# Seven products for the third quarter of an attention output, with block sums, z sums and layer norm scales put elsewhere

## The chip, the cores and the metric

One core of a Trainium2 chip. The metric is the device time of one execution in microseconds (us), the median of several runs; lower is better. TensorE (PE) multiplies matrices, VectorE (DVE) and ScalarE (ACT) do elementwise work, GpSimd (POOL) does some of it too, SyncE (SP) issues the DMAs. The engines run in parallel, each works off its own queue in order, and they wait for each other by semaphores.

## The reference

Four residual layers on x of shape (1, 2048, 1024): attention, GLU, attention, GLU with the same weights in both rounds.

```python
x = x + A(layernorm(x)); x = x + B(layernorm(x))
x = x + A(layernorm(x)); x = x + B(layernorm(x))

# A: 32 heads of 32; phi(t) = where(t > 0, t + 1, exp(t)) + 1e-6
pq, pk = phi(q), phi(k)
kv = einsum("bhsd,bhse->bhde", pk, v); z = einsum("bhsd->bhd", pk)
o = einsum("bhqd,bhde->bhqe", pq, kv) / (einsum("bhqd,bhd->bhq", pq, z)[..., None] + 1e-6)
A = o @ wo
# B: F = 3584
B = (relu(x @ W_gate) * (x @ W_up)) @ W_down
```

## The kernel before

The 2048 tokens are 16 tiles of 128 rows in four quarters of four (QT = 4). The class runs layer_A(0, 1), layer_B(1), layer_A(2, 3), layer_B(3). Layer A makes phi(k), phi(q) and kv, and folds the weight wo into kv (fold_wo): T is then 1024x1024 in bf16, and a tile's attention output is its phi(q), divided by its z sums and transposed (pqT), times T. out_unit (L773) does one tile and one half of the columns: eight matmuls of 128x512 into one bank of the pool `ps` (PSUM, 4 banks), then one DVE instruction (add_up, L768) that adds the residual and gathers the row's sum for the next layer norm. Quarters 0, 1 and 2 go by out_unit, 8 units each, 24 in a layer. Quarter 3 goes by out_pairs (L787): seven block products, Strassen's, for a pair of row tiles against a pair, 56 matmuls in place of 64, with four block sums of T (sums_T, more_T: 128x2048 each) and four of pqT (sums_q: 128x1024). In before they are made while GLU steps u=1 and u=2 of layer B run, and the products follow step u=2.

Around the out stage:

- z sums: for each of 16 tiles z_mult (L723, POOL), z_sum (L728 to L730, DVE: reduce, add, reciprocal), z_scale (L735, POOL), then the transposing DMA q_turn (L744, SP).
- The layer norm of layer B's first half (tiles 0 to 7, ln_norm_sums): L222 on DVE, square, Ln, Exp, shift and scale on ACT (L225 to L231), a transposing DMA (ln_turn, L410), then sums_x (L1127 to L1130, DVE) for four pairs of tiles, which the fifth of the GLU's seven products (`five`, bank vg, L1154) needs.
- make_gu (L1064 to L1067, DVE) makes block sums of a GLU weight; in layer 1 they are stored to DRAM for later (L1068).
- In layer 2 the layer norm's root (ln_root, L173 and L174, ACT) and scale (L180, DVE) lie among the products of q and k.

The order: each unit or product calls later.tick(); later.at(n, f) runs f after n more ticks, and so puts its instructions at that place of the program. In the out stage DVE and POOL keep the program's order (manual_schedule); elsewhere a scheduler orders by its own costs, and issue_after(i) or behind(i, f) keep a step behind instruction i. The order of the out stage in before:

```python
for i in range(11, self.ST):
    later.at(1 + 3 * (i - 11), lambda i=i: z_mult(*divmod(i, QT)))
self.ln_later(last_ln, 0, 2, 2, 2)
run(out0[3:])
for sc in range(1, self.NQ - 1):
    ...
    run(row_major(out_unit, sc))
```

Of the kernel before, what the change touches and what calls it, by code (L numbers as in the profile page):

```python
# [92 lines left out]
class _Net:  # L93
    def __init__(self, tc, ctx, x_d, wqkv_d, wo_d, wg_d, wu_d, wd_d, out_d):
# [23 lines left out]
        self.small = pool("small", 4)  # L118
        self.ps = pool("ps", 4, space=PSUM)
# [64 lines left out]
    def ln_norm(self, layer, t):  # L184
# [14 lines left out]
        def scale(rstd=None if layer == 2 else rstd):  # L199
            if rstd is None:  # L200
                rstd = self.ln_root(mv)
                return lambda: scale(rstd)
# [12 lines left out]
    def ln_norm_sums(self, layer, t):  # L215
# [13 lines left out]
        def scale():  # L229
            nc.scalar.activation(out=shift, in_=mean, func=ACT.Identity, scale=rstd[:, 0:1])  # L230
            nc.scalar.activation(out=xn, in_=src, func=ACT.Identity, scale=rstd[:, 0:1],  # L231
                                 bias=shift[:, 0:1])
            return xn
# [178 lines left out]
    def ln_at(self, delay, layer, t, lag, after=None):  # L412
        def stat():
            with self.tc.issue_after(after) if after else nullcontext():
                scale = self.ln_norm(layer, t)
# [15 lines left out]
    def phi(self, ps, out):  # L431
# [4 lines left out]
        nc.scalar.activation(out=e, in_=e, func=ACT.Exp, scale=-1.0, bias=self.eps6[:, 0:1])  # L436
# [30 lines left out]
    def layer_A(self, l, last_ln):  # L467
# [89 lines left out]
        def m_products(q_first):  # L557
# [39 lines left out]
            later.at(2 if l else 6, lambda: z_chain(0))  # L597
# [118 lines left out]
        def z_chain(i):  # L716
            z_mult(*divmod(i, QT))
            if i < 10:
                later.at(2 + i % 2, lambda: z_chain(i + 1))

        def z_mult(sc, j):
            prod = ksum
            nc.gpsimd.tensor_tensor(out=prod, in0=pq_of[sc, j], in1=zrow, op=ALU.mult)  # L723
            later.at(2, lambda: z_sum(prod, sc, j))

        def z_sum(prod, sc, j):
            den = self.small.tile([P, D // HD], F32, tag="den")
            nc.vector.tensor_reduce(out=den, in_=heads(prod), axis=mybir.AxisListType.X, op=ALU.add)  # L728
            nc.vector.tensor_scalar(out=den, in0=den, scalar1=1e-6 * self.mean, scalar2=None, op0=ALU.add)
            nc.vector.reciprocal(out=den, in_=den)  # L730
            later.at(2, lambda: z_scale(den, sc, j))

        def z_scale(den, sc, j):
# [3 lines left out]
                in1=den[:, :].unsqueeze(2).to_broadcast([P, D // HD, HD]), op=ALU.mult)  # L737
# [49 lines left out]
        def out_pairs(sc):  # L787


            nc, P2 = self.nc, 2 * P  # L790
# [4 lines left out]
            def sums_T():  # L795
                W = self.slot(f"sT{l}", [P, 2, 4, NW], F16)
                S["R"] = R = self.slot(f"sR{l}", [P, 2, 4, NW], F16)
                S[1], S[2], S[4] = W[:, 0], W[:, 1], R[:, 0]
                op(S[1], b12, b11)
                op(f16(b12), b22, b12)  # L800
                later.at(4, more_T)

            def more_T():
                op(S[2], b22, S[1])
                op(S[4], b21, S[2])

            def sums_q():
                q = pqT[sc]
                a11, a12, a21, a22 = (q[:, h:h + 4, i * P2:(i + 1) * P2] for i in range(2) for h in (0, 4))
                s1 = self.temp([P, 4, P2], F16, name="s1")  # L810
                s2, s4 = (S["R"][:, 1, i * 2:i * 2 + 2, :].rearrange("p a (b n) -> p (a b) n", n=P2)
                          for i in range(2))
                op(s1, a21, a22, ALU.add)
                op(s2, s1, a11)
                op(f16(a21), a11, a21)
                op(s4, a12, s2)
                if l == 0:
                    with self.tc.issue_after(self.last_relu.ins):
                        for t in range(sc * QT, sc * QT + QT):
                            for n in range(2):  # L820
                                nc.scalar.activation(out=half(self.x[t], n), in_=half(self.xb[t], n),
                                                     func=ACT.Copy)
# [3 lines left out]
            def products():  # L826
                X = [self.ps.tile([P, NW], F32, tag="a", name=f"ox{i}") for i in range(2)]
                V = [self.ps.tile([P, NW], F32, tag="a", name=f"ov{i}") for i in range(2)]
                Y = [self.ps3.tile([P, NW], F32, tag="b", name=f"oy{i}") for i in range(2)]

                def onto(i, n, bank, last):
                    xs = half(self.x[sc * QT + i], n)
                    if last:
                        add_up(sc * QT + i, n, xs, bank, xs)
                    else:
                        nc.vector.tensor_tensor(out=xs, in0=xs, in1=bank, op=ALU.add)
# [718 lines left out]
```

## Time and profile before

| what | value |
|---|---|
| median of 3 runs | 1448.07 us (1447.98 to 1448.23) |
| profiled execution | 1447.77 us |
| its span, first to last instruction | 1446.0 us |
| granted TensorE clock | 1.000 |
| matmuls | 7430 |
| out stage of layer 0, layer 2 | about 174 to 214 us, 892 to 932 us |

A group's line gives the source line, engine, operation, names, shapes and count, then busy us and mean ns of one, then the idle time before them and what ended it. A window's line gives the stretch, its length, the busy us (and count) of PE, its weight loads, DVE, ACT and POOL, the clock, the DMA share and GB/s. A line of the chain or timeline gives start and duration in us.

### The profile page before, as it was taken

To read this page: it belongs to the slowest core of one execution; us is meant where nothing else is said; L and a number is where in the kernel's file an instruction comes from. 1 tells how busy PE (TensorE), PEld (TensorE's weight loads), DVE (VectorE), ACT (ScalarE), POOL (GpSimd) and SP (SyncE) were. 2 spreads that over 40 slices of the span, in tenths; PEclk is the share of its full clock that TensorE was granted. 3 is DMA by queue.
4 is the path that set the end of the run, shared out by engine and by line. 5 is a ranking of instruction groups with operands and counts; after the bars stand their busy time and mean duration, and the time that the engine had idled before them with its cause. 6 is when DMAs were issued, how large, how long until landed. Compare 5 with 4: busy or idle time off the path is not lost.

```text
span 1446.0 us, 20268 instructions
## 1 busy us (share of the span) xinstructions
PE 1437.7 (99%) x7430; PEld 709.2 (49%) x7430; DVE 959.7 (66%) x1799; ACT 613.8 (42%) x1113; POOL 309.6 (21%) x221
## 2 busy tenths in 40 slices
PE   9999999999999999999999999999999999999998
PEld 4444444444455444445654444444444574444457
DVE  7978698677594456549687885764445864444595
ACT  7872564233334334332168726633333433333300
POOL 1453861011100011110031586410111011111002
PEclk9999999999999999999999999999999999999999
DMA  9950787997469999646973119968644799444465
GB/s 287 237 161 8 176 212 204 288 333 255 162 213 288 355 307 307 202 127 220 297 253 88 58 30 266 261 233 269 217 146 130 220 293 323 146 146 146 153 234 181
DMA packets 328836, 304.90 MB, mean 211 GB/s; under 512 B 107456, under 2 KB 291776, under 8 KB 327712
## 3 DMA queue, kind: packets, MB, share of 16 engines
q1 hardware_dynamic: 320688, 282.30, 65.8%
q10 hardware_dynamic: 6560, 17.24, 3.1%
q0 software_dynamic: 1488, 4.07, 0.8%
q8 instruction: 58, 0.95, 0.3%
q14 instruction: 42, 0.34, 0.1%
HBM read 227.28 MB, written 51.64 MB: 193 GB/s over the span
## 4 chain that ended last, share of the span: by engine, by line
PE 92%; DVE 5%; ACT 1%; issue 1%; DMA 1%; SPq 0%; DVEq 0%; ACTq 0%
PE yu L1154 10%; PE yg L1154 10%; PE ps L493 10%; PE dy L1267 8%; PE xu L1154 6%; PE xg L1154 6%; PE dx L1267 6%; PE ps L776 4%; PE zu L1154 3%; PE vg L1154 3%; PE vu L1154 3%; PE zg L1154 3%; PE my L575 3%; PE dyT L1319 2%; PE mv L575 2%; PE mx L575 2%
## 5 line engine op out<-in xcount | busy, mean ns | idle before, releaser
L1154 PEld LDWEIGHTS <-w 128*128 128x128 f16 (+1 forms) x3136 | 306.7, 98 | 372.4 <-issue 3.6
L1207 POOL TENSOR_TENSOR h<-m5u,m5g 128x512 f16<-128x512 f32 x56 | 72.7, 1298 | 721.1 <-DVE m5u L1203 660.0
L493 PE MATMUL ps<-w,xnT 128*128 128x512 bf16 x768 | 169.9, 379 | 0.5 <-ACT xnT L348 0.3
L1190 DVE TENSOR_TENSOR zg<-yg,m5g 128x512 f32<-128x512 f32 x56 | 39.1, 699 | 180.2 <-PE yg L1154 176.1
L493 PEld LDWEIGHTS <-xnT 128*128 128x128 bf16 x768 | 74.4, 98 | 90.0 <-issue 1.6
L1154 PE MATMUL yg<-s,w 128*128 128x512 f16 x448 | 115.0, 379 | 0.3 <-DVE zg L1190 0.3
L1154 PE MATMUL yu<-s,w 128*128 128x512 f16 x448 | 114.9, 379 | 0.1
L1154 PE MATMUL xu<-xnT,w 128*128 128x512 f16 x448 | 115.0, 379 | 0.0
L1154 PE MATMUL xg<-xnT,w 128*128 128x512 f16 x448 | 115.0, 379 | 0.0
L1267 PEld LDWEIGHTS <-h 128*128 128x128 f16 x672 | 65.7, 98 | 78.3
L1162 ACT ACTIVATE m5g<-m5g 128x512 f32<-128x512 f32 x56 | 35.2, 628 | 155.0 <-DVE m5g L1203 155.0
L1319 PEld LDWEIGHTS <-h 128*128 128x128 f16 x966 | 94.5, 98 | 12.3
L436 ACT ACTIVATE e<-e,eps 128x512 f32<-128x512 f32 x128 | 91.0, 720 | 3.2
L723 POOL TENSOR_TENSOR kvc<-pq,kvc 128x1024 f32<-128x1024 bf16 x32 | 78.5, 2454 | 53.1 <-DVE den L728 32.8
L1267 PE MATMUL dx<-w,h 128*128 128x512 bf16 x392 | 85.3, 379 | 0.0
L776 PE MATMUL ps<-T,pqT 128*128 128x512 bf16 x384 | 83.6, 379 | 0.0
L1171 ACT ACTIVATE m5g<-vg 128x512 f32<-128x512 f32 x56 | 33.4, 597 | 108.5 <-PE vg L1154 108.5
L1165 DVE TENSOR_TENSOR h<-yu,r 128x512 f16<-128x512 f32 x56 | 38.7, 691 | 52.8 <-PE yu L1154 52.8
L514 POOL TENSOR_TENSOR kvc<-kvc,slab 128x512 f32<-128x512 f32 x46 | 57.2, 1249 | 76.0 <-DVE slab L439 72.7
L1162 ACT ACTIVATE r<-yg 128x512 f32<-128x512 f32 x56 | 33.4, 597 | 85.2 <-PE yg L1154 85.2
L1203 DVE TENSOR_TENSOR m5u<-yu,m5u 128x512 f32<-128x512 f32 x56 | 38.7, 690 | 46.3 <-PE yu L1154 46.3
L435 ACT ACTIVATE e<-ps 128x512 f32<-128x512 f32 x92 | 54.2, 589 | 28.9 <-PE ps L493 28.8
(234 smaller groups left out, 2385.5 us busy)
## 6 DMA issues: line engine op xcount, KB each, us to landing
w<-in_B_W_gate_dram SPq DMA_DIRECT2D x56, 512.0 KB, 6.1
w<-in_B_W_up_dram SPq DMA_DIRECT2D x56, 512.0 KB, 6.0
w<-tg SPq DMA_DIRECT2D x42, 512.0 KB, 7.3
w<-tu SPq DMA_DIRECT2D x42, 512.0 KB, 6.6
w<-ddT SPq DMA_DIRECT2D x21, 896.0 KB, 6.5
w<-td SPq DMA_DIRECT2D x18, 896.0 KB, 5.0
w<-dd SPq DMA_DIRECT2D x15, 896.0 KB, 5.0
w<-in_B_W_down_dram SPq DMA_DIRECT2D x14, 896.0 KB, 4.9
```

The source lines that it names most:

```text
L435: nc.scalar.activation(out=e, in_=ps, func=ACT.Relu, scale=-1.0)
L436: nc.scalar.activation(out=e, in_=e, func=ACT.Exp, scale=-1.0, bias=self.eps6[:, 0:1])
L493: nc.tensor.matmul(by_row(ps), lhsT=self.xnT[l, l_q][:, kt, j * P:(j + 1) * P], rhs=w[:, kt, :].rearrange("p (b i d) -> p i b d", i=R, d=H ...
L514: nc.gpsimd.tensor_tensor(out=ksum[:, cols], in0=ksum[:, cols], in1=pk, op=ALU.add)
L575: nc.tensor.matmul(banks[j], lhsT=A(i)[:, j * P:(j + 1) * P], rhs=B(i), start=start and i == 0, stop=i == NS - 1, skip_group_check=True)
L723: nc.gpsimd.tensor_tensor(out=prod, in0=pq_of[sc, j], in1=zrow, op=ALU.mult)
L776: nc.tensor.matmul(ps, lhsT=pqT[sc][:, g, j * P:(j + 1) * P], rhs=T[g // 4][:, g % 4, n2 * NW:(n2 + 1) * NW], start=(g == 0), stop=(g == G ...
L1154: nc.tensor.matmul(ps, lhsT=W[w][m][:, k, :], rhs=A[m][:, k, :], start=start and k == 0, stop=k == 3, skip_group_check=True)
L1162: self.last_relu = nc.scalar.activation(out=out, in_=ps, func=ACT.Relu)
L1207: nc.gpsimd.tensor_tensor(out=h[:, 3, :], in0=V["u"], in1=V["g"], op=ALU.mult)
L1267: nc.tensor.matmul(banks[j], lhsT=A(k)[:, j * P:(j + 1) * P], rhs=w[:, i, :], start=start and k == 0, stop=k == self.U - 1, skip_group_che ...
L1319: nc.tensor.matmul(bank[:, j * H:(j + 1) * H], lhsT=A[i // 2][:, i % 2, j * P:(j + 1) * P], rhs=B[m][:, i, :], start=start and i == 0 and ...
```

## The change

- Quarter 2 also goes by seven products (products(2, 1)) in each attention layer. The order of the products becomes 1, 5, 2, 6, 3, 7, 4. In layer 0 the residual is read from the input tile, with a temporary `held` for one half, in place of copies of x by ACT.
- Three of the block sums of T are made in quarter 0 of the out stage, the fourth ahead of the products; the sums of pqT of quarter 2 in quarter 1.
- The chain of z sums runs from tile 0 to 13; those of tiles 14 and 15 go into the GLU's first step (late_z). Offset and reciprocal are done for two tiles at once.
- The layer norm scale of tiles 4 to 7 is one tensor_scalar on POOL; one of the four sums in sums_x is on POOL for the first half of layers 1 and 3. Tile 7's layer norm is issued behind the products' last copy on ACT.
- make_gu for the first step at ticks 2 and 6 of quarter 1 (3 and 11 before), the later ones apart from each other, their stores behind the last relu. The first GLU step exchanges two pairs of PSUM banks (swap). The transposes and loads of quarter 3 move to u=1 in both layers. The layer norm roots of layer 2 are issued behind the last Exp of phi.

```diff
--- before.py
+++ after.py
...
+        self.den = pool("den", 2)
...
@@ -198,7 +199,8 @@

         def scale(rstd=None if layer == 2 else rstd):
             if rstd is None:
-                rstd = self.ln_root(mv)
+                with self.tc.issue_after(self.last_exp.ins):
+                    rstd = self.ln_root(mv)
                 return lambda: scale(rstd)
...
@@ -227,6 +229,10 @@
         nc.scalar.activation(out=rstd, in_=rstd, func=ACT.Exp, scale=-0.5)

         def scale():
+            if QT <= t < 2 * QT:
+                nc.gpsimd.tensor_scalar(out=xn, in0=src, scalar1=mean, scalar2=rstd[:, 0:1],
+                                        op0=ALU.add, op1=ALU.mult)
+                return xn
...
+            it = after() if callable(after) else after
+            with self.tc.issue_after(it) if it else nullcontext():
...
-        nc.scalar.activation(out=e, in_=e, func=ACT.Exp, scale=-1.0, bias=self.eps6[:, 0:1])
+        self.last_exp = nc.scalar.activation(out=e, in_=e, func=ACT.Exp, scale=-1.0, bias=self.eps6[:, 0:1])

...
-            later.at(2 if l else 6, lambda: z_chain(0))
+            later.at(2 if l else 4, lambda: z_chain(0))
...
@@ -715,26 +722,37 @@

         def z_chain(i):
             z_mult(*divmod(i, QT))
-            if i < 10:
+            if i < self.ST - 3:
                 later.at(2 + i % 2, lambda: z_chain(i + 1))
...
-            later.at(2, lambda: z_sum(prod, sc, j))
+            if (sc, j // 2) == (self.NQ - 1, 1):
+                later.at(2, lambda: self.behind(self.last_z, lambda _: z_sum(prod, sc, j), (0,)))
+            else:
+                later.at(2, lambda: z_sum(prod, sc, j))
+
+        dens = {}

         def z_sum(prod, sc, j):
-            den = self.small.tile([P, D // HD], F32, tag="den")
-            nc.vector.tensor_reduce(out=den, in_=heads(prod), axis=mybir.AxisListType.X, op=ALU.add)
-            nc.vector.tensor_scalar(out=den, in0=den, scalar1=1e-6 * self.mean, scalar2=None, op0=ALU.add)
-            nc.vector.reciprocal(out=den, in_=den)
-            later.at(2, lambda: z_scale(den, sc, j))
+            n, odd = D // HD, j % 2
+            if not odd:
+                dens[sc, j // 2] = self.den.tile([P, 2 * n], F32, tag="den", name="den")
+            den = dens[sc, j // 2]
+            nc.vector.tensor_reduce(out=den[:, odd * n:(odd + 1) * n], in_=heads(prod),
+                                    axis=mybir.AxisListType.X, op=ALU.add)
+            if odd:
+                nc.vector.tensor_scalar(out=den, in0=den, scalar1=1e-6 * self.mean, scalar2=None, op0=ALU.add)
+                nc.vector.reciprocal(out=den, in_=den)
+                for i in range(2):
+                    later.at(2 + 2 * i, lambda i=i: z_scale(den[:, i * n:(i + 1) * n], sc, j - 1 + i))
...
@@ -784,70 +802,72 @@
...
-        def out_pairs(sc):
-
-
...
-            def sums_T():
-                W = self.slot(f"sT{l}", [P, 2, 4, NW], F16)
-                S["R"] = R = self.slot(f"sR{l}", [P, 2, 4, NW], F16)
-                S[1], S[2], S[4] = W[:, 0], W[:, 1], R[:, 0]
-                op(S[1], b12, b11)
-                op(f16(b12), b22, b12)
-                later.at(4, more_T)
-
-            def more_T():
-                op(S[2], b22, S[1])
-                op(S[4], b21, S[2])
-
-            def sums_q():
+            def sums_T(n):
+                if n == 0:
+                    W = self.slot(f"sT{l}", [P, 2, 4, NW], F16)
+                    S["R"] = R = self.slot(f"sR{l}", [P, 2, 4, NW], F16)
+                    S[1], S[2], S[4] = W[:, 0], W[:, 1], R[:, 0]
+                out, a, b = ((S[1], b12, b11), (S[2], b22, S[1]), (S[4], b21, S[2]), (f16(b12), b22, b12))[n]
+                op(out, a, b)
+
+            def sums_q(sc, ns=range(4)):
                 q = pqT[sc]
                 a11, a12, a21, a22 = (q[:, h:h + 4, i * P2:(i + 1) * P2] for i in range(2) for h in (0, 4))
-                s1 = self.temp([P, 4, P2], F16, name="s1")
+                if 0 in ns:
+                    S["s1"] = self.temp([P, 4, P2], F16, name="s1")
+                s1 = S["s1"]
                 s2, s4 = (S["R"][:, 1, i * 2:i * 2 + 2, :].rearrange("p a (b n) -> p (a b) n", n=P2)
                           for i in range(2))
-                op(s1, a21, a22, ALU.add)
-                op(s2, s1, a11)
-                op(f16(a21), a11, a21)
-                op(s4, a12, s2)
-                if l == 0:
-                    with self.tc.issue_after(self.last_relu.ins):
-                        for t in range(sc * QT, sc * QT + QT):
-                            for n in range(2):
-                                nc.scalar.activation(out=half(self.x[t], n), in_=half(self.xb[t], n),
-                                                     func=ACT.Copy)
+                for n in ns:
+                    op(*((s1, a21, a22, ALU.add), (s2, s1, a11), (f16(a21), a11, a21), (s4, a12, s2))[n])
...
-            def products():
+            def products(sc, ticks):
...
-                def onto(i, n, bank, last):
-                    xs = half(self.x[sc * QT + i], n)
-                    if last:
-                        add_up(sc * QT + i, n, xs, bank, xs)
+                held = {}
+
+                def onto(i, n, bank, m):
+                    t = sc * QT + i
+                    xs = half(self.x[t], n)
+                    x0 = half(self.xb[t], n) if l == 0 and m not in (7, 3) else xs
+                    if l == 0 and m == 5:
+                        held[i] = self.temp(name="held")
+                    if m == 7:
+                        x0 = held.get(i, xs)
+                    out = held[i] if i in held and n == 1 else xs
+                    if m in (5, 6):
+                        nc.vector.tensor_tensor(out=out, in0=x0, in1=bank, op=ALU.add)
                     else:
-                        nc.vector.tensor_tensor(out=xs, in0=xs, in1=bank, op=ALU.add)
-
-                for m, bank, start, n in ((1, X, True, None), (5, V, True, (2, 1)), (6, Y, False, (0, 1)),
-                                          (2, X, False, (0, 0)), (7, Y, False, (2, 1)),
-                                          (3, V, False, (0, 1)), (4, Y, False, (2, 0))):
+                        self.last_x = add_up(t, n, out, bank, x0)
+                    if m == 4 and l == 0:
+                        later.at(6, lambda: self.behind(self.last_relu, lambda _: nc.scalar.activation(
+                            out=half(self.x[t], 1), in_=held[i], func=ACT.Copy), (0,)))
+
+                for m, bank, start, n in ((1, X, True, None), (5, V, True, (2, 1)), (2, X, False, (0, 0)),
+                                          (6, Y, False, (0, 1)), (3, V, False, (0, 1)),
+                                          (7, Y, False, (2, 1)), (4, Y, False, (2, 0))):
...
-                            nc.scalar.activation(out=Y[i], in_=X[i], func=ACT.Copy)
+                            self.last_seed = nc.scalar.activation(out=Y[i], in_=X[i], func=ACT.Copy).ins
                         else:
-                            onto(n[0] + i, n[1], bank[i], m not in (5, 6))
-                        later.tick()
+                            onto(n[0] + i, n[1], bank[i], m)
+                        if i or ticks == 2:
+                            later.tick()
...
@@ -943,27 +963,31 @@
...
-            for i in range(11, self.ST):
-                later.at(1 + 3 * (i - 11), lambda i=i: z_mult(*divmod(i, QT)))
+            sums_T, sums_q, products = out_pairs()
+            for n, at in enumerate((1, 3, 5)):
+                later.at(at, lambda n=n: self.behind(self.last_x, sums_T, (n,)))
             self.ln_later(last_ln, 0, 2, 2, 2)
             run(out0[3:])
             for sc in range(1, self.NQ - 1):
                 if sc == 1:
                     for j in range(QT):
-                        self.ln_at(2 * j + 2, last_ln, QT + j, 2)
-                        later.at((11 if l else 12, 13, 15, 16)[j], lambda j=j: self.sums_x(last_ln, 0, j))
-                if sc == 2 and l:
-                    for j in range(QT):
-                        later.at(11 + j, lambda j=j: q_turn(self.NQ - 1, j))
-                    for t in range(self.ST - QT, self.ST):
-                        later.at(3 + t, lambda t=t: self.behind(self.last_turn, bring, (t,)))
+                        self.ln_at((2, 4, 6, 9)[j], last_ln, QT + j, 2, lambda j=j: self.last_seed if j == 3 else None)
+                        later.at((11 if l else 12, 13, 15, 16)[j], lambda j=j: self.behind(
+                            self.last_x, lambda j: self.sums_x(last_ln, 0, j), (j,)))
                 if sc == 1 and l == 0:
-                    for w, n in (("g", 3), ("u", 11)):
+                    for w, n in (("g", 2), ("u", 6)):
                         later.at(n, lambda w=w: self.behind(
                             self.last_x, lambda w: self.make_gu(ring.get((last_ln, 0, w, 0)), w, 0), (w,)))
-                run(row_major(out_unit, sc))
-            self.pairs = out_pairs(self.NQ - 1)
-            self.turns = [] if l else [lambda j=j: q_turn(self.NQ - 1, j) for j in range(QT)] + [
+                if sc == 1:
+                    for n in range(4):
+                        later.at(3 + n, lambda n=n: self.behind(self.last_x, lambda n: sums_q(2, (n,)), (n,)))
+                    run(row_major(out_unit, sc))
+                else:
+                    self.behind(self.last_x, sums_T, (3,))
+                    products(sc, 1)
+            self.pairs = lambda: sums_q(self.NQ - 1), lambda: products(self.NQ - 1, 2)
+            self.late_z = [lambda j=j: z_mult(self.NQ - 1, j) for j in (2, 3)]
+            self.turns = [lambda j=j: q_turn(self.NQ - 1, j) for j in range(QT)] + [
                 lambda t=t: self.behind(self.last_turn, bring, (t,)) for t in range(self.ST - QT, self.ST)]


...
-        self.later.at(3, lambda: self.nc.scalar.dma_start(
-            out=self.tgu[w, u], in_=t[:, 4:8, :].bitcast(F16)))
+
+        def store():
+            with self.tc.issue_after(self.last_relu.ins) if u else nullcontext():
+                self.nc.scalar.dma_start(out=self.tgu[w, u], in_=t[:, 4:8, :].bitcast(F16))
+
+        self.later.at(3, store)
...
-        v.tensor_tensor(out=s3, in0=a11, in1=a21, op=ALU.subtract)
+        self.last_s3 = (self.nc.gpsimd if c == 0 and l % 2 else v).tensor_tensor(out=s3, in0=a11, in1=a21, op=ALU.subtract)
         v.tensor_tensor(out=s4, in0=a12, in1=s2, op=ALU.subtract)
...
+        swap = c == 0 and u == 0
+
+        def bank(w, third, name):
+            if third:
+                return self.ps3.tile([P, NW], F32, tag="b", name=name)
+            return self.kvp.tile([P, NW], F32, tag="kv0" if w == "g" else "kv1", name=name)
+
         def five(w):
-            v = self.kvp.tile([P, NW], F32, tag="kv0" if w == "g" else "kv1", name=f"v{w}")
+            v = bank(w, swap, f"v{w}")
             mm(w, 5, v, True)
...
-            Y[w] = self.ps3.tile([P, NW], F32, tag="b", name=f"y{w}")
+            Y[w] = bank(w, not swap, f"y{w}")
...
-                        self.later.at(4 if u else 9, lambda u=u: behind(self.last_put if u else self.last_z, lambda: [
-                            self.make_gu(ring.get((l, c, w, u + 1)), w, u + 1) for w in "gu"]))
+                        for n, w in enumerate("gu"):
+                            self.later.at((4 if u else 9) + 4 * n, lambda u=u, w=w: behind(
+                                self.last_put if u else self.last_z,
+                                lambda: self.make_gu(ring.get((l, c, w, u + 1)), w, u + 1)))
...
+                if c == 0 and u == 0:
+                    for n, z in enumerate(self.late_z):
+                        self.later.at(7 + 3 * n, lambda z=z: behind(self.last_s3, z))
                 if c == 0 and u == 1:
                     for n, turn in enumerate(self.turns):
-                        self.later.at(1 + n, turn)
-                if c == 0 and u in (1, 2):
-                    self.later.at(6, lambda u=u: behind(self.last_put, self.pairs[u - 1]))
+                        self.later.at(7 + n + 6 * (n // QT), turn)
+                if c == 0 and u == 2:
+                    self.later.at(6, lambda: behind(self.last_put, self.pairs[0]))
                 self.glu(l, c, u, hT)
                 if c == 0 and u == 2:
-                    self.pairs[2]()
+                    self.pairs[1]()
...
```

More of the change, by code (lines that the diff above doesn't have):

```diff
@@ L413, in stat @@
         def stat():
-            with self.tc.issue_after(after) if after else nullcontext():
+            it = after() if callable(after) else after
+            with self.tc.issue_after(it) if it else nullcontext():
                 scale = self.ln_norm(layer, t)
@@ L736, in z_scale @@
                 out=heads(pq), in0=heads(pq),
-                in1=den[:, :].unsqueeze(2).to_broadcast([P, D // HD, HD]), op=ALU.mult)
+                in1=den.unsqueeze(2).to_broadcast([P, D // HD, HD]), op=ALU.mult)
             if sc < self.NQ - 1:
@@ L784, in out_unit, with out_pairs @@
             self.last_x = add_up(t, n2, xs, ps, x0)
-        def out_pairs(sc):
-            nc, P2 = self.nc, 2 * P
+        def out_pairs():
+            P2 = 2 * P
             f16 = lambda a: a.bitcast(F16)
```

## The prediction

> **What bounds the kernel now.** I read the page's busy lines and chain first, then windows over the stages the change touches (layer 0: 174 to 222 us, layer 2: 890 to 938), then the groups of instructions there by shape, the timeline where a group's mean looked wrong, and the chain again at PE's few stalls. The page:
>
> ```profile
> span 1446.0 us, 20268 instructions
> ...
> PE 1437.7 (99%) x7430; PEld 709.2 (49%) x7430; DVE 959.7 (66%) x1799; ACT 613.8 (42%) x1113; POOL 309.6 (21%) x221
> ...
> PE 92%; DVE 5%; ACT 1%; issue 1%; DMA 1%; SPq 0%; DVEq 0%; ACTq 0%
> ```
>
> TensorE is busy all but 8 us, so a matmul removed is time removed, provided that no other engine becomes late in that stage. The windows (span in us, then busy us of PE, PEld, DVE, ACT and POOL) show how near that is:
>
> ```profile
> 174.00:192.00 18.00, 18.00 (x96) 8.11 (x88) 15.54 (x39) 11.17 (x22) 17.38 (x9) 1.00 0.80 178
> 192.00:209.00 17.00, 17.00 (x80) 7.70 (x79) 16.19 (x35) 15.60 (x32) 12.20 (x7) 1.00 0.78 185
> 209.00:222.00 13.00, 12.76 (x59) 5.58 (x58) 11.43 (x32) 2.96 (x5) 0.00 (x0) 1.00 1.06 241
> 890.00:910.00 20.00, 20.00 (x107) 8.88 (x106) 13.62 (x38) 13.76 (x27) 11.09 (x7) 1.00 1.12 271
> 910.00:925.00 15.00, 15.00 (x71) 6.83 (x70) 11.46 (x32) 14.81 (x31) 10.91 (x7) 1.00 1.11 256
> ```
>
> DVE is busy 31.7 of the 35 us from 174 to 209, POOL 97% of the first window: in layer 0 there is hardly room on DVE, in layer 2 some. What fills them, DVE and then POOL, 174 to 222 us:
>
> ```profile
> L768 DVE SCALAR_TENSOR_TENSOR x<-ps,x 128x512 f32<-128x512 f32 x24 | 15.9, 669 | 1.5 <-PE ps L776 1.1
> L728 DVE TENSOR_REDUCE den<-kvc 128x32 f32<-128x1024 f32 x7 | 8.5, 1214 | 0.1
> L1064 DVE TENSOR_TENSOR w<-w 128x1024 f16<-128x1024 bf16 x2 | 4.5, 2256 | 0.0
> ...
> L735 POOL TENSOR_TENSOR pq<-pq,den 128x1024 bf16<-128x1024 bf16 x8 | 15.3, 1911 | 0.7 <-DVE den L730 0.7
> L723 POOL TENSOR_TENSOR kvc<-pq,kvc 128x1024 f32<-128x1024 bf16 x7 | 14.9, 2127 | 5.9 <-DVE den L728 5.9
> ```
>
> The same L1064, and the block sums that the change moves, 222 to 250 us:
>
> ```profile
> L1064 DVE TENSOR_TENSOR w<-w 128x1024 f16<-128x1024 bf16 x6 | 3.9, 683 | 0.0
> ...
> L546 DVE TENSOR_TENSOR sT<-T 128x2048 f16<-128x2048 bf16 x1 | 1.2, 1219 | 0.0
> ...
> L546 DVE TENSOR_TENSOR s<-pqT 128x1024 f16<-128x1024 bf16 x1 | 0.7, 682 | 0.0
> ```
>
> One shape, 0.68 us in one place and 2.26 in the other. The timeline says why:
>
> ```profile
> 192.39 1.91 POOL L735 TENSOR_TENSOR pq<-pq,den 128x1024 bf16<-128x1024 bf16 x1
> 192.47 2.38 DVE L1064 TENSOR_TENSOR w<-w 128x1024 f16<-128x1024 bf16 x1
> ```
>
> The DVE sum ends 0.55 us after POOL's multiply ends (194.30): it did not move until then. The other one (206.93, 2.13 us) lies over POOL's 206.61 to 208.52 in the same way. Reduces (1214 ns) and additions out of PSUM (669) under POOL are not longer than alone.
>
> Last, the stalls of PE. The chain from 748 to 755 us in layer 2:
>
> ```profile
> 749.14 0.29 ACT rstd L173
> ...
> 750.01 0.67 ACT e L436
> ...
> 752.06 1.02 PE qy L677 x4
> ```
>
> PE lost 1.19 us before 752.06 (distance of matmul starts over their usual 0.216). An Ln of a layer norm, waiting for its mean, held ACT and with it the exponential that DVE and PE needed. At 217.83 PE lost another 0.40, at vg, waiting for L1127 of tile 7.
>
> [...] The two-input multiplies of 128x1024 take 1.91 and 2.12 here; no row shows a one-input operation on POOL.
>
> **The change part by part.**
> *Seven products.* Eight units of eight matmuls become 56: eight fewer per layer. Eight take 1.727 us (pitch 215.8 ns), so −1.73 twice, −3.45. This is the sure part. DVE's results become 12 of 0.61 in place of 8, 2.4 us more, after unit 16.
>
> *The DVE queue of layer 0 up to unit 16.* The first addition starts at 175.7. An addition costs 0.61 with its accumulator read (the chain gives 1.22 for two). To the end of the 16th: 16 additions 9.8; four reduces at 1.14 4.6; two merged offset-and-reciprocal pairs on 64 columns 1.7 (0.19 and 0.35 on 32; between 1.1 and 1.8); seven L222 at 0.2 1.4; make_gu g and u, (0.68+0.42+0.42) each, 3.0; three block sums of T at 1.22 3.7; four of pqT at 0.68 2.7. Sum 26.9, with 0.8 of idle (before had 2.0 with less work) 27.7: end 203.4. The same sum for before is 23.0 + 2.3 of waits for POOL + 2.0 idle = 27.3, which its 16th addition at 203.0 confirms. PE finishes unit 16 at 200.16, and the fifth product's second half, 202.75 at the earliest, needs the bank of addition 16. So even without any wait for POOL PE stalls about 0.65.
>
> *Waits for POOL.* Three T sums and four pqT sums join the two L1064, all with two SBUF inputs, each apart from the others behind an addition. The last pqT sum follows L1067 directly; the other eight meet POOL. The first four lie where POOL is 95% busy with instructions of 2 us: mean rest 1.0, 3.8 together. The others meet it at 50 to 60%: z sums 14 and 15 have gone, but four LN scales come in: 2.2. Together 6.0, bounds 0 (DVE always gets in between two POOL instructions, as L1066 and L1067 did at 194.9) and 8 (nearly the whole rest each time). I take 6.0, as both isolated cases on record waited, 1.70 and 1.45. Addition 16 ends at 209.4, PE loses 6.65.
>
> *Behind it.* PE: products 5, 2, 6, 3, 7, 4 from 209.4 less the half already done, 9.5 us, and the four GLU products ahead of vg 3.45: vg at 222.3. DVE beside it: b12 1.22, 12 results 7.3, 12 sums of x (S3 is now on POOL) about 5.0, 0.4: s1 of tile 7 at about 221.6, just hidden. Product 4 stands directly behind 7 on the same banks, which DVE has to read in between: 0.2. The LN scale on POOL is 1.1 (as ACT's L231) to 2.1 (as L723); I take 1.6. The 0.40 stall at vg goes. Layer 0: +6.65 +0.2 −1.73 −0.40 = +4.7; bounds −1.3 and +6.7.
>
> *Layer 2.* There is no make_gu, so DVE has 23.9 us of work in 27.6 of PE's. But the three T sums and 4.3 of waits (0.25, 0.7, 1.45 and 1.9, from where POOL's rows of before would stand) fall into units 4 to 10; four banks let PE be ahead by four units, and it loses about 2.3 at units 11 to 13. +2.3 −1.73 = +0.6; bounds −1.7 and +1.5.
>
> *Layer norm roots of layer 2* issue behind the last exponential: the stall at 752.06 goes, −1.0, bounds −1.3 and 0 (the scales L180 on DVE, 0.80 each, may land in front of another product).
>
> *The rest.* make_gu split in two and later stores: small GLU stalls of 0.1 to 0.5, −0.3 (−0.6 to 0). T sums out of u=1: 4.9 us of DVE in a GLU where it had room, nothing. x copies go from ACT, nothing (ACT is 42% busy). Late z sums 14 and 15, turns and loads of quarter 3: their user is the products behind u=2, over 25 us on; SP's weight loads land in about 6 us and are issued five ahead; nothing.
>
> Sum +4.7 +0.6 −1.0 −0.3 = +4.0. The profiled execution took 1447.77, 1.8 of it outside the span; the median is 1448.07, so 1452.1.
>
> **Rivals.**
> *DVE gets in between* (faster): POOL's and DVE's instructions interleave so that hardly a sum waits. For: L1066 and L1067 waited for nothing; the z chain starts earlier, so POOL may be idle sooner. Against: 97% busy POOL. −1.3 −1.7 −1.2 −0.3 = −4.5: 1443.6. It turns into mine at the point where the eight sums wait over 4 us together.
> *Half the waits* (no change): 3.0 in layer 0, stall 3.65: +1.7; layer 2 −0.6; −1.3: −0.2, 1447.9.
> *Layer norm of tile 7* (slower still): its L222 stands behind the late b12, then square 1.2, roots 0.8, POOL's scale 1.6 to 2.1 with up to 1.2 of waiting for DVE, transpose 3.6 and s1. From 210.9 that gives 219 to 221, under 222.3; one more tick or POOL instruction in front pushes vg to 224: 1453.8. For: the scale shares POOL with z work. Against: the present slack of 1 to 3 us.
> That the seven products remove nothing is excluded by the count of matmuls.
>
> **How the numbers follow.** Forecast 0.40, half 0.20, no waits 0.30, tile 7 0.10. A measurement of this kernel tells 0.2%, 2.9 us, from no change. Faster 0.34 (no waits and a part of half), same 0.17, slower 0.49. Range 1443.6 (no waits) to 1455.8 (layer 0 at +6.7 with layer 2 at +1.5 and little gained elsewhere); the forecast's own is 1450 to 1455.8.
>
> **What would show it.** Right: T and pqT sums of 1.5 to 3 us ending half a us or one us after a POOL row; PE stalls between 192 and 210 of 5 to 7 us, released by L768; 7414 matmuls; no stall at qy near 750. Wrong: these sums at 1.22 and 0.68, additions ending by 204, and vg before 217. Then the matmuls' 3.45 appear in full.

## The result, and the profile after

The changed kernel takes 1466.26 us (1465.86 to 1467.51, four runs) against 1448.03 for before, measured with it: a ratio of 1.0127, 95% interval 1.011 to 1.0145. It is slower, as forecast, but by 18.2 us where 4 were forecast, and outside the range.

The page of the changed kernel (the numbers of lines are now those of the changed file: L786 for L768, L794 for L776, L862 for the products, L1155 to L1158 for the sums of x, L1182 for L1154):

```profile
span 1464.7 us, 20206 instructions
...
PE 1437.1 (98%) x7387; PEld 707.7 (48%) x7414; DVE 977.5 (67%) x1775; ACT 603.0 (41%) x1097; POOL 335.8 (23%) x237
```

There are 7414 weight loads, 16 fewer than before, so the matmuls did go (some matmul records are missing from this trace). Yet PE's busy time is almost unchanged, and its idle time, span less busy, is up by 19 us. The windows say where (us of the stretch, then busy us of PE, its loads, DVE, ACT, POOL, then PE's clock):

```profile
174.00:192.00 18.00, 17.88 (x93) 8.18 (x95) 16.38 (x29) 8.45 (x18) 14.58 (x7) 1.00 0.67 152
192.00:209.00 17.00, 11.39 (x50) 4.76 (x49) 16.54 (x32) 12.55 (x27) 10.83 (x7) 1.00 0.86 192
209.00:224.00 15.00, 10.69 (x49) 4.79 (x49) 14.76 (x27) 3.28 (x7) 9.46 (x7) 1.00 0.62 155
224.00:228.00 4.00, 4.00 (x12) 1.47 (x11) 2.36 (x9) 0.64 (x2) 0.00 (x0) 0.57 0.00 0
...
921.00:935.00 14.00, 11.78 (x54) 5.24 (x54) 13.44 (x32) 11.39 (x27) 7.22 (x4) 1.00 1.11 320
935.00:950.00 15.00, 10.51 (x48) 4.52 (x47) 13.10 (x22) 3.98 (x11) 9.89 (x8) 1.00 1.07 245
```

Two separate losses in each layer: PE idles ahead of the products (192 to 209), and again among them (209 to 224), where DVE is 98% busy (in layer 2 from 921 and from 935, with DVE at 96% and 87%). From 224 to 228 PE is never idle and yet slow: its granted clock is 0.57. What PE waited for, summed over the run (total, times, longest):

```profile
PE ps L794 <- DVE x L786: 5.2, 5, 1.7
PE oy L862 <- DVE held L786: 3.8, 1, 3.8
PE oy L862 <- DVE x L786: 2.6, 1, 2.6
PE ov L862 <- DVE x L786: 1.8, 1, 1.8
PE oy L862 <- DVE x L850: 1.6, 1, 1.6
```

The five longest are all waits for DVE. The sixth, 1.5 us in two waits, is for ACT's copy of product 1; in layer 0 it cost nothing by itself, since the fifth product behind it had to wait until 209.49 for a bank that DVE was still reading. The longest single wait is product 4's, for the addition (`held`) that reads product 7's bank. Setting the starts of the same matmuls side by side in both traces, with a stall counted as the distance of two starts over 0.216 us, gives this account:

| stretch | forecast | measured | made of |
|---|---|---|---|
| layer 0 to the GLU's vg | +4.7 | +10.5 | stalls to the fifth product 7.1, product 4 3.9, slow clock 1.7, vg's old stall −0.4, matmuls −1.7 |
| the first GLU steps of layer 1 | part of −0.3 | +2.6 | 1.19 and 1.42, others cancel |
| layer norm roots, layer 2 | −1.0 | −0.9 | 1.19 and 0.28 at qy and qx gone, 0.34 and 0.27 new |
| layer 2 from the out stage to the GLU | +0.6 | +5.7 | units 2.5, product 2 (for ACT's copy of product 1) 0.4, products 7 and 4 1.8 and 2.8, matmuls −1.7 |
| the rest | 0 | +0.5 | 0.3 in the first GLU step of layer 3, 0.1 ahead of the out stage |

The timeline shows how the second loss comes about. DVE and then POOL, layer 0:

```profile
215.07 1.00 DVE L1155 TENSOR_TENSOR s<-xnT 128x512 f16<-128x512 f16 x1
216.11 1.26 DVE L1156 TENSOR_TENSOR s<-s,xnT 128x512 f16<-128x512 f16 x1
217.40 1.26 DVE L1158 TENSOR_TENSOR s<-xnT,s 128x512 f16<-128x512 f16 x1
...
219.81 2.23 DVE L1155 TENSOR_TENSOR s<-xnT 128x512 f16<-128x512 f16 x1
222.07 0.42 DVE L1156 TENSOR_TENSOR s<-s,xnT 128x512 f16<-128x512 f16 x1
```

```profile
214.64 5.04 POOL L1157 TENSOR_TENSOR s<-xnT,xnT 128x512 f16<-128x512 f16 x4
219.64 2.12 POOL L730 TENSOR_TENSOR kvc<-pq,kvc 128x1024 f32<-128x1024 bf16 x1
```

The last line of DVE's is what such a sum costs alone: 0.42. The first three ran in turns with four GpSimd instructions, 1.26 apiece; the fourth lay under the z multiply of tile 14. The change itself put both of these on GpSimd at this place. And the chain of waits carries it to PE:

```profile
219.88 2.17 DVE s L1155
...
222.95 0.62 DVE held L786 x2
223.57 0.04 issue
223.61 1.58 PE oy L862 x5
```

The sums of x stood ahead of the read of product 7's bank in DVE's queue, and product 4 writes that bank.

### The profile page after: what moved, and what is told of

It is laid out like the page before. It is cut to its first block, busy times and chain, and to the rows that moved or that the text cites. A ratio compares the mean times of both kernels' runs of the same rounds, so it can differ in the third digit from the quotient of the medians.

```text
span 1464.7 us, 20206 instructions
## 1 busy us (share of the span) xinstructions
PE 1437.1 (98%) x7387; PEld 707.7 (48%) x7414; DVE 977.5 (67%) x1775; ACT 603.0 (41%) x1097; POOL 335.8 (23%) x237
## 4 chain that ended last, share of the span: by engine, by line
PE 89%; DVE 5%; ACT 2%; issue 1%; DMA 1%; SPq 1%; POOL 0%; DVEq 0%; ACTq 0%
PE ps L500 10%; PE yu L1182 10%; PE yg L1182 10%; PE dy L1302 7%; PE xu L1182 6%; PE xg L1182 6%; PE dx L1302 6%; PE vu L1182 3%; PE zg L1182 3%; PE vg L1182 3%; PE zu L1182 3%; PE my L582 2%; PE dyT L1354 2%; PE mv L582 2%; PE mx L582 2%; PE dy L1354 2%
## 5 line engine op out<-in xcount | busy, mean ns | idle before, releaser
L1182 PEld LDWEIGHTS <-w 128*128 128x128 f16 (+1 forms) x3136 | 306.8, 98 | 375.9 <-issue 8.0
L1182 PE MATMUL yg<-s,w 128*128 128x512 f16 x448 | 115.0, 379 | 1.3 <-DVE zg L1225 1.3
L1182 PE MATMUL xg<-xnT,w 128*128 128x512 f16 x448 | 115.9, 380 | 0.0
L1182 PE MATMUL xu<-xnT,w 128*128 128x512 f16 x448 | 115.5, 380 | 0.0
L1182 PE MATMUL yu<-s,w 128*128 128x512 f16 x448 | 114.9, 379 | 0.1
L753 POOL TENSOR_TENSOR pq<-pq,den 128x1024 bf16<-128x1024 bf16 x32 | 66.6, 2084 | 5.1 <-DVE den L747 4.0
L1190 ACT ACTIVATE r<-zg 128x512 f32<-128x512 f32 x56 | 32.8, 585 | 81.5 <-PE zg L1182 77.8
```

The lines of the kernel that those rows point to most:

```text
L753: nc.gpsimd.tensor_tensor(out=heads(pq), in0=heads(pq), in1=den.unsqueeze(2).to_broadcast([P, D // HD, HD]), op=ALU.mult)
L1182: nc.tensor.matmul(ps, lhsT=W[w][m][:, k, :], rhs=A[m][:, k, :], start=start and k == 0, stop=k == 3, skip_group_check=True)
L1190: self.last_relu = nc.scalar.activation(out=out, in_=ps, func=ACT.Relu)
```

## The experiments

Theory A: DVE's instructions with two SBUF inputs wait for GpSimd's, and all of the loss follows from that. Theory B: the change gives DVE too much work of its own. Beside each time stands the median of before that was measured with it. A stall of PE is again the distance of two starts over 0.216 us.

**GpSimd's z work left out.** Tiles 8 to 15 get neither z multiply nor z scale on GpSimd; DVE keeps its part.

```diff
-            nc.gpsimd.tensor_tensor(out=prod, in0=pq_of[sc, j], in1=zrow, op=ALU.mult)
+            if sc < 2: nc.gpsimd.tensor_tensor(out=prod, in0=pq_of[sc, j], in1=zrow, op=ALU.mult)
...
-            nc.gpsimd.tensor_tensor(
+            if sc < 2: nc.gpsimd.tensor_tensor(
                 out=heads(pq), in0=heads(pq),
```

> The changed kernel with GpSimd's z multiply and z scale of tiles 8 to 15 left out in both attention layers (outputs of those tokens are not the reference's; DVE keeps its reduces and reciprocals). Theory A, DVE's two-input sums wait for GpSimd instructions: the T sums come back to 1.22 us and the GLU weight sums to 0.68; the 5 stalls up to the fifth product in layer 0 (7.1 us together) shrink by about 5.5, product 4's stall and the slow clock behind it by 3, the two stalls in the first GLU steps (1.19 and 1.42) go, layer 2 gains about 4: some 15 us in all, about 1451. Theory B, DVE has simply too much work of its own: the sums stay long or the additions stay late, and the time stays within 2 us of 1466.

Measured: 1448.98 (before 1448.51; ratio 1.0002, 0.9993 to 1.001), 17 us less than the changed kernel, with every DVE instruction still there. The moved sums in the groups of DVE, 174 to 230 us, first of the changed kernel:

```profile
L553 DVE TENSOR_TENSOR sR<-T,sT 128x2048 f16<-128x2048 bf16 x1 | 2.8, 2751 | 0.0
L553 DVE TENSOR_TENSOR sT<-T 128x2048 f16<-128x2048 bf16 x1 | 2.6, 2606 | 0.0
...
L553 DVE TENSOR_TENSOR sT<-T,sT 128x2048 f16<-128x2048 bf16 x1 | 1.5, 1470 | 0.0
```

and then of this one:

```profile
L553 DVE TENSOR_TENSOR sT<-T,sT 128x2048 f16<-128x2048 bf16 x1 | 1.2, 1220 | 0.0
L553 DVE TENSOR_TENSOR sR<-T,sT 128x2048 f16<-128x2048 bf16 x1 | 1.2, 1220 | 0.0
L553 DVE TENSOR_TENSOR sT<-T 128x2048 f16<-128x2048 bf16 x1 | 1.2, 1160 | 0.0
```

These sums read nothing that the z work writes, so no dependence can explain their length. Leaving the z work out also takes away waits of DVE's reduces for GpSimd's products, but DVE is busy 32.8 of the 35 us from 174 to 209 in this run and 32.9 in the changed kernel: it did not stand idle for them. The stalls up to the fifth product fell from 7.1 to 1.1 us and the two in the GLU went. What is left at product 4 is 2.12 in layer 0 and 1.49 in layer 2, with the third sum of x still on GpSimd. Theory B falls as the cause of these 17 us.

**The third sum of x on DVE.**

```diff
-        self.last_s3 = (self.nc.gpsimd if c == 0 and l % 2 else v).tensor_tensor(out=s3, in0=a11, in1=a21, op=ALU.subtract)
+        self.last_s3 = v.tensor_tensor(out=s3, in0=a11, in1=a21, op=ALU.subtract)
```

> The changed kernel with the third sum of x back on DVE. Theory A: the sums of x no longer alternate with GpSimd (1.0 and 1.26 us each in the changed kernel), so a batch takes 4 x 0.42 = 1.7 in place of 3.6 us although it has one sum more; product 4's stall of 3.9 in layer 0 falls to about 2, the 1.8 and 2.8 of layer 2 to 0 and 2: about -5 us, 1461. Theory B: DVE gets 1.7 us more in each layer and the time rises by 1 to 2, 1468.

Measured: 1458.66 (before 1448.51; ratio 1.007, 1.0055 to 1.0086), 7.6 less, with four sums more on DVE in each of the two layers. Its timeline, DVE:

```profile
216.02 0.42 DVE L1155 TENSOR_TENSOR s<-xnT 128x512 f16<-128x512 f16 x1
216.47 0.42 DVE L1156 TENSOR_TENSOR s<-s,xnT 128x512 f16<-128x512 f16 x1
216.81 0.42 DVE L1157 TENSOR_TENSOR s<-xnT,xnT 128x512 f16<-128x512 f16 x1
217.15 0.42 DVE L1158 TENSOR_TENSOR s<-xnT,s 128x512 f16<-128x512 f16 x1
```

Four sums in 1.5 us, where three took 3.6. Product 4's stall of 3.9 in layer 0 is gone entirely, and in layer 2 the 1.8 and 2.8 are 0.3 and 0.7. One reason why the gain is more than the 5 expected is that the z multiply of tile 14 moved as well. With the third sum off GpSimd it ran at 195.4 in place of 219.6 (in layer 2 at 917.0 in place of 945.0), ahead of the products and not over the second batch:

```profile
195.43 2.14 POOL L730 TENSOR_TENSOR kvc<-pq,kvc 128x1024 f32<-128x1024 bf16 x1 [0.17 <-DVE den L743]
```

So this run doesn't separate the third sum from the z multiply, and part of the cost went elsewhere: at 201.3 a unit now waits 2.79, where it waited 1.85, and the slow clock follows that stall.

**Both together.** The two edits above in one kernel; of GpSimd's work beside the out stage only the four layer norm scales are left.

> GpSimd's z multiply and z scale of tiles 8 to 15 left out and the third sum of x on DVE, in one kernel: of GpSimd's work beside the out stage only the four layer norm scales stay. If waiting for GpSimd is the whole of the loss, DVE's own work fits and the removed matmuls appear: the stalls that were left without z (2.1 and 1.5 us at product 4) go too, about 1445, 3 below before. If DVE's work is too much by itself, the stall at the fifth product (1.1) grows and the time stays at 1448 to 1449.

Measured: 1445.3 (before 1448.54; ratio 0.9978, 0.997 to 0.9986). DVE's own work, products and all, fits: two stalls over half a us remain in the out stage of layer 0 (1.09 at the fifth product, 0.76 at vg), none in that of layer 2. The removed matmuls appear: 3.45 for them and 1.3 for the layer norm roots (measured alone below), less 1.09 and less the 0.36 that vg waits longer than in before, is 3.3, and 3.2 were measured. The windows of this kernel beside those of the changed one hold the surprise:

```profile
174.00:192.00 18.00, 17.78 (x95) 8.08 (x94) 16.32 (x36) 10.48 (x20) 0.00 (x0) 1.00 1.09 240
192.00:209.00 17.00, 16.02 (x74) 7.22 (x74) 16.51 (x39) 12.53 (x30) 5.20 (x4) 1.00 0.77 160
```

DVE is as busy as in the changed kernel (16.38 and 16.54), but it completes 75 records where it completed 61. In these profiles the wait for GpSimd is counted as busy time of the DVE instruction that waits.

**Product 3 between 7 and 4.**

```diff
-                                          (6, Y, False, (0, 1)), (3, V, False, (0, 1)),
-                                          (7, Y, False, (2, 1)), (4, Y, False, (2, 0))):
+                                          (6, Y, False, (0, 1)), (7, Y, False, (2, 1)),
+                                          (3, V, False, (0, 1)), (4, Y, False, (2, 0))):
```

> The changed kernel with the products in the order 1, 5, 2, 6, 7, 3, 4, so that product 3 stands between 7 and 4. If product 4 is late because DVE's read of product 7's bank stands behind the sums of x, then that read comes where that of product 3 was, product 4 starts about 3.7 us sooner in layer 0, and the next limit is the last sum of x ahead of the fifth GLU product: about -3 in layer 0 and -1.2 in layer 2, 1462. If the layer norm of tile 7 alone sets the start of the GLU's sums, nothing changes (within 1 us).

Measured: 1463.73 (before 1448.51; ratio 1.0102, 1.0088 to 1.0116), 2.5 less. In layer 0 product 4's stall shrinks from 3.94 to 1.23, as expected; in layer 2 product 7 now waits 2.63 for DVE in its place. The trace also has two stretches of slow clock where the changed kernel has one, about 1.7 us more. The order of the products decides which of them meets the sums of x, not whether one does.

**Quarter 2 by units again, the other moves kept.** The lines not shown make the fourth T sum with those of quarter 3, and take the layer norm of tile 7 out from behind the products' copy, which isn't there.

```diff
-                if sc == 1:
-                    for n in range(4):
-                        later.at(3 + n, lambda n=n: self.behind(self.last_x, lambda n: sums_q(2, (n,)), (n,)))
-                    run(row_major(out_unit, sc))
-                else:
-                    self.behind(self.last_x, sums_T, (3,))
-                    products(sc, 1)
+                run(row_major(out_unit, sc))
```

> The changed kernel with quarter 2 by eight-matmul units again (its four sums of pqT are not made, the fourth T sum is made with those of quarter 3); every other move of the change stays. Theory A: the moved T sums, the GpSimd scales and sums still meet each other: 3.45 us of matmuls come back, the stalls at product 4 go, the stalls before it stay in part: about 1456, 8 above before. Rival: only the products' own results on DVE made it late, and without them the moves cost nothing: 1447, as before less the 1.3 of the layer norm roots.

Measured: 1459.89 (before 1448.42; ratio 1.0081, 1.0066 to 1.0096). So the moves without the products cost 11.5 us (and 1.3 more, since the gain of the layer norm roots is in it), more than the 8 expected and far from nothing: the unit stalls (0.79, 0.90, 1.85, 1.61) stay, and the first GLU products wait for additions that stand behind the sums of x (1.76).

**The layer norm scale of tiles 4 to 7 on ACT.**

```diff
-            if QT <= t < 2 * QT:
+            if t < 0:
                 nc.gpsimd.tensor_scalar(out=xn, in0=src, scalar1=mean, scalar2=rstd[:, 0:1],
```

> The changed kernel with the layer norm scale of tiles 4 to 7 back on ACT. Theory A: the waits of the pqT and GLU weight sums for these four GpSimd instructions (0.4 + 0.8 + 0.9 in layer 0) go: about -2, 1464. Rival: ACT's 1.5 us for each tile come back on the path to the last sums of x and nothing is won, 1466.

Measured: 1461.11 (before 1448.42; ratio 1.0091, 1.0076 to 1.0106), 5.2 less than the changed kernel and more than the 2 expected. The product 4 stalls are gone in both layers: in layer 0 the third sums now come one by one, and the first six DVE sums of x take 0.41 to 0.42 each. But in layer 2 product 2 waits 2.7 for ACT's copy of product 1, which now stands behind ACT's scales, and in layer 0 a unit waits 3.43 where it waited 1.85. The profiled execution is the slowest of the four, 2 us over the median. Which part of the gain is the wait for GpSimd and which is the new order of DVE was not separated.

**All z sums of quarter 3 in the GLU**, with the third sum of x on DVE.

```diff
-            if i < self.ST - 3:
+            if i < self.ST - 5:
...
-            self.late_z = [lambda j=j: z_mult(self.NQ - 1, j) for j in (2, 3)]
+            self.late_z = [lambda j=j: z_mult(self.NQ - 1, j) for j in range(4)]
...
-                        self.later.at(7 + 3 * n, lambda z=z: behind(self.last_s3, z))
+                        self.later.at(6 + 3 * n, lambda z=z: behind(self.last_s3, z))
```

> The third sum of x on DVE, and the z sums of all four tiles of quarter 3 (12 to 15), not two, in the first GLU step. Against the run with the sum on DVE alone (1458.7): DVE loses two reduces and a reciprocal pair (3.3 us) in the out stage, and two of the T sums and a GLU weight sum find GpSimd idle (3.5 us of waits): the stalls up to the fifth product fall from 7 to about 1 in layer 0, from 2 to 0.5 in layer 2; two more z sums meet the GLU weight sums in the first GLU steps (+1.5). About 1450. If the T sums wait for something else than GpSimd: no better than 1455.

Measured: 1467.83 (before 1448.42; ratio 1.013, 1.0113 to 1.0147), a miss by 18 us. The out stage of layer 0 is as hoped (vg at 218.25, stalls of 1.9, 0.3 and 0.3). But the GLU pays it back: 1.1, 2.4, 0.9, 3.0 and 3.1 in its first steps, where DVE makes the GLU weight sums while POOL does the z sums, and about 3 more from two stretches of slow clock behind these stalls. In layer 2 product 7 waits 3.6, with another such stretch. DVE, then POOL:

```profile
242.59 1.53 DVE L1091 TENSOR_TENSOR w<-w 128x512 f16<-128x512 bf16 x1
244.05 2.39 DVE L1088 TENSOR_TENSOR w<-w 128x1024 f16<-128x1024 bf16 x1
246.37 0.69 DVE L1225 TENSOR_TENSOR zu<-yu,m5u 128x512 f32<-128x512 f32 x1
```

```profile
241.88 4.01 POOL L753 TENSOR_TENSOR pq<-pq,den 128x1024 bf16<-128x1024 bf16 x2 [3.09 <-DVE den L747]
```

Two weight sums (0.42 and 0.68 alone) become 3.9 us in front of an addition for which PE waits. In layer 3 there are no weight sums and the four z sums still cost 0.9, 1.8 and 1.8: their reduces (1.2 each) and a tensor_scalar that waits (1.73) stand in DVE's queue ahead of what PE needs. So waiting for GpSimd is not all of what late z sums cost.

**T sums later as well.**

```diff
-            for n, at in enumerate((1, 3, 5)):
+            for n, at in enumerate((5, 8, 12)):
```

> The same, and the first three T sums later in the out stage (5, 8 and 12 ticks in place of 1, 3 and 5), where GpSimd has finished with tiles 8 to 11. Theory A: each at 1.22 us, another 1 to 2 us gained, 1448.5 to 1449. Rival: they now crowd DVE ahead of the products, and the fifth product waits: 1 to 2 slower than with the z sums alone.

Measured: 1461.83 (before 1448.42; ratio 1.0093, 1.0077 to 1.0108). The 1448.5 to 1449 expected was missed for the same reason as in the run before (GLU stalls of 1.1, 2.4, 2.3 and 3.1), but the later T sums gained 6 us over it, most in layer 2, where the stall of 3.6 at product 7 went. There the three T sums are at 1.22 each, as expected; in layer 0 only one is, the others took 1.96 and 1.87.

**Layer norm roots alone, on the kernel before.**

```diff
-                rstd = self.ln_root(mv)
+                with self.tc.issue_after(self.last_exp.ins):
+                    rstd = self.ln_root(mv)
```

> The kernel before with one part of the change alone: the layer norm roots of layer 2 issued behind the last Exp of phi. As in the prediction the stall of 1.19 at qy near 752 us goes: -1.0, 1447.0. Rival: the scales on DVE come in front of another product and the time is the same within 0.3.

Measured: 1447.21 against 1448.51 (ratio 0.999, 0.9984 to 0.9997): 1.3 less, and the stall at qy is gone. This kernel leaves nothing out and is faster than before and than the changed kernel.

**The change in layer 2 alone**, with the third sum of x on DVE; layer 0 gets the units, z order, ticks, T sums and scales of before back by conditions on the layer (the central one below), and keeps the merged reciprocals, the exchanged banks and the `held` copies.

```diff
-                if sc == 1:
-                    for n in range(4):
+                if sc == 2 and l == 0:
+                    run(row_major(out_unit, sc))
+                elif sc == 1:
+                    for n in range(4 if l else 0):
```

> The change in layer 2 alone (quarter 2 by seven products, early T sums, two late z sums, GpSimd scales for layer 3), with the third sum of x on DVE; layer 0 keeps units, z order, ticks and ACT scales of before. From the run with that sum on DVE (its layer 2 lost 3.3 us in stalls for 1.73 of matmuls): +1.4 there, -1.3 for the layer norm roots: 1448 to 1449, as before. If layer 2's loss was in truth handed on from layer 0: 1445.5.

The second one has its T sums at ticks 5, 8 and 12.

> The same with the T sums of layer 2 at ticks 5, 8 and 12 in place of 1, 3 and 5, where fewer GpSimd instructions are left: the stalls of 0.9 and 0.8 in the units go, unless DVE is then late at the fifth product; 1447 to 1447.5, about what the layer norm roots alone give. Rival: no gain, 1449.

Measured: 1451.18 (ratio 1.0017, 1.001 to 1.0025) and 1451.32 (1.002, 1.0013 to 1.0027), before 1448.46. Both are above what was expected. From vg to vg, layer 2 lost 1.9 by itself in the first, with the gain of the layer norm roots taken out. That is near the 1.4 expected, so its loss is not handed on from layer 0. The later T sums take the unit stalls away and put 0.8 and 1.4 at the fifth product instead; they still met GpSimd and took 2.06, 2.61 and 1.75. Layer 0 came out about 2 us later than before, in part since the GLU's second product waits 1.1 for a bank; why that was not pursued.

## Why the prediction was right and wrong

- *Seven products, −3.45.* Right by the count of weight loads, and visible in the time only where GpSimd is out of the way: 1445.3, which holds the 1.3 of the layer norm roots too.
- *The DVE queue up to unit 16.* Right, and not by luck: addition 16 was forecast to end at 209.4 and ended at 210.3; PE's loss was put at 6.65 and was 7.1. The sums waited 6.4 us where 6.0 were forecast: 3.2 in the three T sums, 2.9 in the GLU weight sums and 0.4 in one sum of pqT, each against its length alone. That they waited for GpSimd is shown by leaving its z work out: the T sums are back at 1.22, 1.22 and 1.16.
- *Behind it: the failed step.* The prediction put the waits of PE behind unit 16 at 0.2 us: "12 sums of x (S3 is now on POOL) about 5.0", "just hidden", and the 0.2 for product 4. The sums were priced at 0.42 each, as in before, where POOL is idle at that place (0.00 busy from 209 to 222). The change puts two things there: the third sum and the z multiply. The first four sums of x on DVE took 1.00, 1.26, 1.26 and 2.23 in place of 1.7 together: 4.1 us of wait, 2.3 of them for the third sums and 1.8 for the z multiply. Product 4 stood behind them, by 3.94; the slow clock added 1.7. With the z work out 2.12 of the 3.94 remained, and with the third sum on DVE as well nothing. The waits had been counted for the sums ahead of unit 16 and not for those behind it.
- *Layer 2, +0.6.* The units' part was right (2.3 forecast, 2.5 measured); products 7 and 4 (1.8 and 2.8) are the same missed term again: there the first four sums of x on DVE took 1.17, 1.26, 1.25 and 2.32. With layer 0, the missed term and the slow clock are 10.0 of the 14.2 us that the forecast lacked.
- *Layer norm roots, −1.0.* Right: −0.9 in the changed kernel, −1.3 alone.
- *The rest, −0.3, late z sums at nothing.* Wrong: 2.6 us in layer 1. The z multiply and scales meet GLU weight sums, which took 1.75 and 1.53 in place of 0.42 and 2.39 in place of 0.68, and the z reduces add 1.2 each. Late z sums of four tiles cost 10.5 us of stalls there.
- *Rivals.* "DVE gets in between" and "Half the waits" fall with the 6.4 us of wait up to unit 16; with GpSimd's work away DVE does fit (1445.3). The layer norm of tile 7 did not decide: with the sum on DVE, vg comes 3.9 us sooner with the same scale on GpSimd.

## What to carry to other kernels

Work given to GpSimd was not taken off DVE here, because DVE had instructions with two SBUF inputs at the same time: each waited for the other's to end, and the wait looked like busy time (sums of x took 1.26 us each beside the third sums, 0.42 alone; a z scale that began at 184.38, while DVE's T sum ran until 185.51, took 2.90, the one at 180.43 took 1.91). Before moving anything to GpSimd, list the two-input DVE instructions in its new neighbourhood, and who waits behind each of them in DVE's queue. A stretch that is quiet in the old profile is only quiet until the change itself fills it.

## What was not expected of the hardware

After product 4's wait PE ran at half its pitch. Its operations from 223 to 229 us:

```profile
223.61 2.86 PE L862 MATMUL oy<-sR,pqT 128*128 128x512 f16 x8 [3.77 <-DVE held L786]
226.27 1.06 PE L1182 MATMUL xg<-xnT,w 128*128 128x512 f16 x2
227.12 1.36 PE L1182 MATMUL xu<-xnT,w 128*128 128x512 f16 x4
228.32 1.03 PE L1182 MATMUL vg<-s,w 128*128 128x512 f16 x4
```

Starts lie 0.43 us apart until 227.9, then 0.216 again; 1.7 us are lost beyond the stall. Each stretch at half clock in the traces, but for those cut off by the end of an execution, lasts 3.41 us (in one run two follow each other), and all changes of the clock in a run lie whole multiples of 3.41 us apart. PE need not be idle for all of the period before: ahead of this fall it was busy for 0.77 us of it. Windows of the changed kernel, cut at these places:

```profile
207.31:210.72 3.41, 1.58 (x8) 0.68 (x7) 3.27 (x8) 0.69 (x2) 1.43 (x2) 1.00 0.79 157
220.96:224.38 3.42, 0.77 (x4) 0.38 (x4) 3.14 (x7) 0.00 (x0) 0.79 (x1) 1.00 0.13 32
224.38:227.79 3.41, 3.41 (x10) 1.18 (x8) 1.98 (x6) 0.43 (x1) 0.00 (x0) 0.50 0.00 0
944.59:948.00 3.41, 1.77 (x9) 0.69 (x7) 3.34 (x5) 0.58 (x1) 2.53 (x2) 1.00 1.00 337
```

With the traces of all runs cut so, start and end of the execution left out, and PE's idle time in a period taken from the distance of its starts, the clock fell ten times. The period before held 2.07 to 3.30 us of idle time each time; no period with 2.04 or less was followed by a fall, and none with more went without. In the changed kernel it was 2.65 us in the period from 220.96, and 1.99 in the longest without a fall behind it, from 207.31. That is the limit in these thirteen traces, not a measured law. By it the length of a stall alone doesn't tell whether the clock falls. The changed kernel's stall of 2.8 at 949 is cut in two at 948.00 and has no fall behind it. The run with product 3 moved has a stall of 2.0 that lies in one period with the end of another, 2.07 together, and the clock falls. The stretch in the changed kernel cost 1.7 us, half its length, with PE at work throughout; with the same behind a stall of 2.0 us, an estimate from these two figures, such a stall costs nearly twice what it lasts.

A tensor_scalar on 128x64 waits as well: 2.10 us under a z multiply in the kernel with all z sums in the GLU, and 0.64 at 181.76 in the changed kernel, where a z scale ends at 182.34; it takes 0.18 to 0.20 where GpSimd is not in the way. The prediction counted waits of instructions with two SBUF inputs alone, and this one has one. Reduces (1.20 to 1.22) and additions out of PSUM (0.63 to 0.69) kept their length beside GpSimd, in before and in the changed kernel.
